# One full-height subtraction below block 0, later masks, another order of SyncE's DMAs and an inverse from blocks of 8 rows, in a delta-rule attention kernel with a feed-forward layer

## The chip, the cores and the metric

The kernel runs on one core of a Trainium2 chip. The metric is the device time of one execution in microseconds (us). Each kernel is run several times and the median is taken; a profiled execution beside them gives the trace. Engines are named as in the profile: PE (matmuls), PEld (its weight loads), DVE (vector), ACT (scalar), POOL (GpSimd), SP (SyncE, which here only issues DMAs).

## The reference

Two layers, one after the other: a delta-rule attention over 4 batches x 8 heads, 768 positions of 48 elements, then a feed-forward layer with a quick GELU on 3072 tokens of 384 elements (the heads side by side) with 2048 hidden units.

```python
k_n = k / (norm(k) + 1e-06)
for t in range(S):
    y[:, :, t] = einsum('bhd,bhde->bhe', q[:, :, t], state)
    v_old = einsum('bhde,bhd->bhe', state, kt)
    state = state + bt * einsum('bhd,bhe->bhde', kt, vt - v_old)
...
h = x @ w_in
g = h * (1.0 / (1.0 + exp(-1.702 * h)))
out = g @ w_out
```

q, k, v and beta are float32. The two weight matrices arrive as 8-byte floats, and the kernel turns them into float32 on the chip.

## The kernel before, in words

**Tiling.** The sequence is cut into 6 chunks of 128 positions; a unit is one chunk of one batch (24 units, 8 heads each). Within a chunk the recurrence is a triangular system: with G the products of the keys among each other, U solves a unit lower triangular system with right side V. The chunk is cut into 4 blocks of 32 rows. `invert` (line 441) computes the inverses XB of the 32 x 32 diagonal blocks for all heads at once on DVE; then a unit's solve goes block by block: `solve` (623) forms U of a block (psU), `solved` (630) copies it out on ACT (US<-psU), `below` (610) multiplies it by G into the rows below (psR), `rest` (619) subtracts that from V on DVE (V<-V,psR). For block 0 `rest` makes two subtractions, 32 rows and 64 rows[...].

**Inverse.** It works in two 16-row halves: 15 rounds (line 471) of a multiply (P<-NT,YB) and a reduce (YB<-P) build the inverse of both halves at once, then eight larger multiply-reduce pairs (489, 498) build the block between them. Chunk 0 gets its input NT from PE over a transpose; chunk 1 gets it over DRAM: `prepare` (402) writes 32-column blocks of G to a buffer Nd in DRAM with four DMAs per unit, and reads them back as NT with one; both are on SP's queue. The first multiply of chunk 1's inverse is NT<-NT,bI. The inverse of chunk 0 ends with a transpose (YT) and four multiplies into XB; that of later chunks goes back through DRAM (Yd, XB<-Yd).

**Scores.** `scores` (565) turns q, multiplies with the keys (psQ), copies the result to M on ACT, and `select` (604) sets its upper triangle to zero on POOL with an affine select over 128 x 1024 elements ("mask" below).

**Order.** Most instructions are pinned to program order on their engine (the wrapper at line 102, which is why the profile gives line 102 for them). The parts of the start are interleaved by hand:

- lines 928-957, chunk 0: turned keys, norms, G, the inverse begun as a generator (947) and run at 952, 32 scalings of V on ACT (955, V<-V,zs), and the four masks (957). `warm(n)` (132) issues n dummy matmuls (ps_warm) that keep PE busy; `warm(NY)` inside the inverse (501) waits for a memset that DVE issues there.
- lines 994-1001, first pair of chunk 0's units: `hops` (959) yields calls of `together` (803), each a solve of one unit beside the product below of the other: (a,0); (b,0) with a's block 0; (a,1) with b's block 0; and so on. After each call come some steps of the weight conversion (`fill`, 294), a step of `preparing` (`keys`, 972: norms, turned keys, G and Nd/NT for chunk 1) and dummies.
- lines 1002-1009: outputs of the pair (`put_out`), then q and v loads of units 4 and 5 on SP.
- lines 1025-1039, second pair: the same, with `feed` (1013) giving PE parts of the feed-forward layer (`hidden`, 707: ph) in place of dummies after the third hop.
- lines 1045-1064: scores of unit 4 (V<-V,psQ among them), the rest of the `w_in` conversion, chunk 1's inverse (1057) with parts of ph between, then `w_out` conversions.
- line 1066: the steady part, `woven` (847), one step per unit, with feed-forward work taken from a queue.

The conversion (205) of a piece is five instructions on DVE and a Relu on ACT: a `tensor_scalar` into `w_in` or `w_out`, one into `tmp`, and three `scalar_tensor_tensor`. The feed-forward matmuls of a piece wait for it.

Of the kernel before, what the change touches and what calls it, by code (L numbers as in the profile page):

```python
# [18 lines left out]
def kernel(  # L19
# [32 lines left out]
    HB = 2  # L52
# [2 lines left out]
    GB = 8  # L55

    XR = DP - D
    NW, NA, NY, NU = 14, 3, 46, 11
    NQ = DFF // 4
    NPC = DFF // 8  # L60
    NS = C * C + C
# [67 lines left out]

    ones = ident.bitcast(mybir.dt.bfloat16)  # L130

    def warm(n, after=None):
        ps = ps_moe.tile([128, 256], F32, tag="moe", name="ps_warm")
        if after is not None:
            after(ps[:, 0:1], 0.0)
        for _ in range(n):
            pe.matmul(ps, lhsT=ones[:, 0:128], rhs=ones, start=True, stop=True)

# [263 lines left out]
    def prepare(n):  # L402

        c, b = units[n]
        turn(n)
        yield 0.6
        G = gram(n)
        if c == 1:
            Nd = dram.tile([H * C * BS], F32, tag="Nd", name="Nd", bufs=4)
            for blk in range(NB):  # L410
                u = slice(blk * BS, (blk + 1) * BS)
                sync(out=Nd.rearrange("(h p k) -> p h k", p=C, k=BS)[u], in_=G[u, :, u])
            yield 0.9
            sync(
                out=NT[b * NB * H : (b + 1) * NB * H].rearrange("d i k -> d (i k)"),
                in_=Nd.rearrange("(d r) -> d r", r=BS * BS),
            )
            yield 0.0
            return
        Nd = dram.tile([H * NS], F32, tag="Nd", name="Nd", bufs=4)  # L420
        dma = sync if c < 3 else nc.sync.dma_start
        dma(
            out=Nd.rearrange("(h r) -> h r", r=NS)[:, 0 : C * C].rearrange(
                "h (p k) -> p h k", k=C
            ),
            in_=G,
        )
        dma(
            out=NT[b * NB * H : (b + 1) * NB * H],
            in_=Nd.rearrange("(d r) -> d r", r=NS // NB)[:, 0 : BS * C].rearrange(  # L430
                "d (i k) -> d i k", k=C
            )[:, :, 0:BS],
        )
        yield 0.9
# [6 lines left out]
    def invert(c, b0=0, nb=B):  # L441

        np = nb * NB * H
        part = slice(b0 * NB * H, b0 * NB * H + np)
        N, Y = NT[part], YB[part]
        bc = bI[part, c].broadcast_to([np, BS, BS])
        tt, red = vec.tensor_tensor, vec.tensor_reduce
        if c > 0:
            tt(N, N, bc, op=ALU.mult)
            yield 0.0  # L450
        HS = BS // 2

        def dots(o, a, b, ny, nx, nk, negate):

            P = wk.tile([128, ny, nx, nk], F32, tag="P", name="P")[part]
            tt(P, a, b, op=ALU.mult)
            red(o, P, axis=AX.X, op=ALU.add, negate=negate)

        def halves(t):

            return [t[:, s * HS : (s + 1) * HS, s * HS : (s + 1) * HS] for s in range(2)]


        Yf = Y.rearrange("p j i -> p (j i)")
        Nf = N.rearrange("p i k -> p (i k)")
        step = HS * BS + HS

        def diag(t, off, dims):
            return bass.AP(t.tensor, t.offset + off, [t.ap[0], [step, 2]] + dims)

        for i in range(1, HS):
            P = wk.tile([128, 2, i, i], F32, tag="P", name="P")[part]
            tt(
                P, diag(Nf, i * BS, [[0, i], [1, i]]), diag(Yf, 0, [[BS, i], [1, i]]),
                op=ALU.mult,
            )
            red(diag(Yf, i, [[BS, i]]), P, axis=AX.X, op=ALU.add, negate=True)
            yield 0.0


        X1 = N[:, 0:HS, HS:]
        if c <= 1:
            vec.tensor_copy(X1, halves(Y)[1].rearrange("p l i -> p i l"))
        else:
            act.activation(X1, halves(Y)[1].rearrange("p l i -> p i l"), ACT.Copy)
        A = N[:, 0:HS, 0:HS]
        N10, Y0 = N[:, HS:, 0:HS], halves(Y)[0]
        Q = 4
        for j in range(0, HS, Q):
            n = HS - j  # L490
            dots(
                A[:, j : j + Q, :],
                N10[:, :, j:].rearrange("p (o l) k -> p o l k", o=1).broadcast_to([np, Q, HS, n]),
                Y0[:, j : j + Q, j:].rearrange("p j (o k) -> p j o k", o=1).broadcast_to([np, Q, HS, n]),
                Q, HS, n, False,
            )
            yield 0.0
        for i in range(0, HS, Q):
            n = i + Q
            if c == 0 and i == HS - 3 * Q:  # L500
                warm(NY, vec.memset)
            dots(
                Y[:, 0:HS, HS + i : HS + i + Q],
                A[:, :, 0:n].rearrange("p j (o l) -> p j o l", o=1).broadcast_to([np, HS, Q, n]),
                X1[:, i : i + Q, 0:n].rearrange("p (o i) l -> p o i l", o=1).broadcast_to([np, HS, Q, n]),
                HS, Q, n, True,
            )
            yield 0.0
        if c == 0:
            T = wk.tile([128, BS, BS], F32, tag="P", name="YT")  # L510
            vec.transpose(T.rearrange("p d i -> p i d"), Y.rearrange("p j i -> p i j"))
            for b in range(B):
                XB = wk.tile([128, H, BS], F32, tag="XB", name="XB", bufs=4)
                tt(
                    XB, T[:, b * H : (b + 1) * H],
                    zs[:, 5, b].broadcast_to([128, H, BS]), op=ALU.mult,
                )
                inverse[b] = XB
                yield 0.0
            return  # L520
        YS = wk.tile([128, BS, BS], F32, tag="P", name="YS")[part]
        tt(YS, Y, bc, op=ALU.mult)
        dma = sync if c < 3 else nc.sync.dma_start
        groups = [range(b0, b0 + nb)]
        back = {}
        for bs in groups:
            for b in bs:
                back[b] = dram.tile([H * C, BS], F32, tag="Yd", name="Yd", bufs=4)
                dma(
                    out=back[b].rearrange("(p j) i -> p j i", j=BS),  # L530
                    in_=YS[(b - b0) * NB * H : (b - b0 + 1) * NB * H],
                )
            for b in bs:
                XB = wk.tile([128, H, BS], F32, tag="XB", name="XB", bufs=4)
                dma(out=XB, in_=back[b].rearrange("(h t) i -> t h i", h=H))
                inverse[c * B + b] = XB
        yield 0.0
# [7 lines left out]
    class Step:  # L545
# [63 lines left out]

        def below(self, blk, h, psR):  # L610
            r = slice(blk * BS, (blk + 1) * BS)
            for k in range(blk + 1, NB):
                u = slice(k * BS, (k + 1) * BS)
                pe.matmul(
                    psR[u, h, :], lhsT=self.G[r, h, u], rhs=self.U[r, h, :],
                    start=True, stop=True,
                )

        def rest(self, blk, psR):
            for u in (slice(BS, 2 * BS), slice(2 * BS, C)) if blk == 0 else (slice((blk + 1) * BS, C),):  # L620
                vec.tensor_tensor(self.V[u], self.V[u], psR[u], op=ALU.subtract)

        def solve(self, blk, h, psU):
            r = slice(blk * BS, (blk + 1) * BS)
# [328 lines left out]
    for s in pair:  # L953
        for h in range(H):
            act.mul(s.V[:, h, :], s.V[:, h, :], zs[:, 4, s.b, h : h + 1])
    for s in pair:
        s.select()

    def hops(a, b):

# [11 lines left out]
    def keys():  # L972

        def unit(n):
            yield from normalize_mixed(n)
            yield from prepare(n)

        begun[2 * B] = prepare(2 * B)

        def first(n):  # L980
            yield from normalize_mixed(n)
            next(begun[n])

        work = [unit(n) for n in range(B, 2 * B)] + [first(2 * B)]
        for t in range(22):
            for u, begin in enumerate((0, 3, 6, 10, 13)):
                s = t - begin
                if s >= 0 and s % 2 == 0:
                    next(work[u], None)
            yield  # L990
        for w in work:
            run(w)
# [2 lines left out]
    path = hops(*pair[:2])  # L995
    for i in range(2 * NB):
        together(*next(path))
        fill(1 if i < 2 else 2)
        if i > 0:
            ahead_of(preparing, 1)  # L1000
        warm(NU if i < 6 else NA)
    for n, s in enumerate(pair[:2]):
        put_out(s, 2 - n)
        load(len(KN) + n, ((KN, k),), other_queue)
        fill(1 + n)
    for n in range(B, B + 2):
        load(n, ((QP, q),), sync)
    for n in range(B, B + 2):
        load_values(n, sync)

    ffn = []

# [13 lines left out]
    for i in range(2 * NB):  # L1026
# [6 lines left out]
        ahead_of(preparing, 2)  # L1033
        if 3 <= i < 6:
            fetch_out(i - 3)
    for s in pair[2:]:
        put_out(s, 2)
        feed()
        fill(1)
    ffn.append(hidden(xTs[1], gTs[1], slice(0, NTH), 1.3, True))  # L1040
    xTs.pop(0), xTs.pop(1)
    load(B + 2, ((QP, q),), sync)
    for n in range(2 * B + 1, 2 * B + 1 + HB):
        load(n, ((KN, k),), sync)
# [55 lines left out]
```

## Time and profile before

| | us |
|---|---|
| median of 3 runs | 775.84 |
| lowest, highest | 775.49, 777.72 |
| the profiled execution | 775.34 |
| its span | 773.6 |
| PE busy | 747.1 (97% of the span) |
| DVE busy | 455.2 (59%) |
| ACT, POOL busy | 241.5, 126.5 |
| 96 subtractions V<-V,psR on DVE | 53.3 |
| 165 dummies ps_warm on PE | 23.6 |
| 20 masks M<-M on POOL | 25.4 |

The mean granted clock of PE was 0.976 of full speed. A busy time is the sum of the durations of an engine's instructions; PE's are modelled, so a full PE is not PE at its peak. A group's row gives the output and input tiles, partitions x elements, the count, the busy time, the mean duration of one in ns, and the idle time of the engine ahead of it with what ended it. The chain of waits goes back from the last instruction to what released each step. "issue" in it is time for which the profile shows no cause. Float32 matmuls appear as two records, called passes below.

### The profile page before, as it was taken

To read this page: it belongs to the slowest core of one execution; us is meant where nothing else is said; L and a number is where in the kernel's file an instruction comes from. 1 tells how busy PE (TensorE), PEld (TensorE's weight loads), DVE (VectorE), ACT (ScalarE), POOL (GpSimd) and SP (SyncE) were. 2 spreads that over 40 slices of the span, in tenths; PEclk is the share of its full clock that TensorE was granted. 3 is DMA by queue.
4 is the path that set the end of the run, shared out by engine and by line. 5 is a ranking of instruction groups with operands and counts; after the bars stand their busy time and mean duration, and the time that the engine had idled before them with its cause. 6 is when DMAs were issued, how large, how long until landed. Compare 5 with 4: busy or idle time off the path is not lost.

```text
span 773.6 us, 18836 instructions
## 1 busy us (share of the span) xinstructions
PE 747.1 (97%) x8165; PEld 560.1 (72%) x8165; DVE 455.2 (59%) x935; ACT 241.5 (31%) x535; POOL 126.5 (16%) x132
## 2 busy tenths in 40 slices
PE   7898999789999999999999999999999999999997
PEld 6677788456688678678678678678678677686774
DVE  6989879996975675665665665666665621000000
ACT  4564642343333223223223233233223123121110
POOL 6314200010220320220221211221210000000000
PEclk8598999999999999999999999999999999999999
DMA  9946640644342142042042042042030020000000
GB/s 167 176 65 174 145 87 1 170 114 97 76 109 56 25 105 56 22 107 57 22 101 63 22 100 65 22 97 66 22 77 13 22 44 2 16 12 1 25 1 21
DMA packets 130658, 50.73 MB, mean 66 GB/s; under 512 B 105408, under 2 KB 126016, under 8 KB 130576
## 3 DMA queue, kind: packets, MB, share of 16 engines
q1 hardware_dynamic: 128112, 41.08, 24.5%
q0 software_dynamic: 2464, 8.46, 4.5%
q8 instruction: 64, 1.05, 0.6%
q14 instruction: 18, 0.15, 0.1%
HBM read 32.08 MB, written 16.25 MB: 62 GB/s over the span
## 4 chain that ended last, share of the span: by engine, by line
PE 80%; DVE 14%; issue 2%; DMA 2%; ACT 2%; SPq 0%; POOL 0%; DVEq 0%; POOLq 0%; ACTq 0%
PE po L102 29%; PE ph L102 26%; PE psY L102 6%; PE psU L102 5%; PE psQ L102 4%; PE psG L102 4%; PE psT L102 3%; DVE P L102 3%; DVE w_out L102 2%; DVE tmp L102 2%; DVE YB L102 2%; PE psR L102 2%; PE ps_warm L102 2%; DVE V L102 1%; DVE NT L102 1%
## 5 line engine op out<-in xcount | busy, mean ns | idle before, releaser
L102 PE MATMUL po<-w_out,gT 128*128 128x384 f32 x768 | 266.1, 494 | 7.4 <-DVE w_out L102 7.4
L102 PE MATMUL ph<-xT,w_in 128*128 128x256 f32 x1152 | 261.2, 383 | 0.3
L102 PEld LDWEIGHTS ph<-xT,w_in 128*128 128x128 f32 x1152 | 214.8, 190 | 32.6 <-issue 1.7
L102 PEld LDWEIGHTS po<-w_out,gT 128*128 128x128 f32 x768 | 141.1, 190 | 98.8 <-DVE w_out L102 9.1
L102 DVE TENSOR_TENSOR V<-V,psR 64x384 f32<-64x384 f32 (+1 forms) x96 | 53.3, 555 | 189.8 <-PE psR L102 186.8
L102 ACT ACTIVATE gT<-ph 128x512 f32<-128x512 f32 x96 | 56.5, 596 | 142.3 <-PE ph L102 142.2
L102 DVE TENSOR_TENSOR P<-NT,YB 64x8 f32<-64x8 f32 (+31 forms) x190 | 89.4, 470 | 5.4
L102 ACT COPY US<-psU 32x384 f32<-32x384 f32 x92 | 43.2, 470 | 134.7 <-PE psR L102 120.5
L102 DVE TENSOR_REDUCE YB<-P 64x4 f32<-64x8 f32 (+31 forms) x190 | 80.9, 426 | 6.5
L102 PEld LDWEIGHTS psU<-V,XB 32*32 32x32 f32 x1536 | 57.7, 105 | 36.5 <-issue 27.7
L102 PE MATMUL psU<-V,XB 32*32 32x48 f32 x1536 | 68.6, 203 | 3.2 <-DVE V L102 2.4
L605 POOL TENSOR_SCALAR_AFFINE_SELECT M<-M 128x1024 f32<-128x1024 f32 x20 | 25.4, 1268 | 231.4 <-DVE M L102 167.4
L102 PE MATMUL psR<-US,G 32*32 32x48 f32 x2208 | 60.0, 203 | 0.6 <-ACT US L102 0.6
L102 PEld LDWEIGHTS psR<-US,G 32*32 32x32 f32 x2208 | 50.7, 105 | 1.9 <-ACT US L102 0.7
L102 PE MATMUL psQ<-QS,kT 48*128 48x176 f32 (+1 forms) x384 | 37.6, 341 | 3.0 <-ACT QS L102 3.0
L102 PE MATMUL psG<-kT 48*128 48x128 f32 x384 | 32.4, 306 | 3.4 <-ACT kT L102 2.2
L102 PEld LDWEIGHTS psQ<-QS,kT 48*128 48x128 f32 x384 | 31.1, 209 | 6.2 <-ACT QS L102 5.1
L102 DVE TENSOR_TENSOR P<-NT 64x256 f32<-64x256 f32 (+7 forms) x40 | 34.3, 859 | 0.4
L102 DVE TENSOR_REDUCE NT<-P 64x64 f32<-64x1024 f32 (+7 forms) x40 | 32.6, 815 | 1.4
L102 PEld LDWEIGHTS psG<-kT 48*128 48x128 f32 x384 | 27.4, 205 | 6.8 <-ACT kT L102 2.6
L102 ACT COPY o<-po 128x384 f32<-128x384 f32 x24 | 11.5, 479 | 61.7 <-issue 39.2
L102 ACT COPY M<-psQ 128x256 f32<-128x256 f32 x68 | 22.8, 376 | 22.7 <-DVE V L102 16.0
(99 smaller groups left out, 600.9 us busy)
## 6 DMA issues: line engine op xcount, KB each, us to landing
Nd<-G SPq DMA_DIRECT2D x16, 512.0 KB, 3.5
QP<-in_q_dram SPq DMA_DIRECT2D x24, 192.0 KB, 4.3
V<-in_v_dram SPq DMA_DIRECT2D x24, 192.0 KB, 3.1
out_dram<-o SPq DMA_DIRECT2D x24, 192.0 KB, 2.6
KN<-in_k_dram POOLq DMA_DIRECT2D x15, 192.0 KB, 3.6
NT<-Nd SPq DMA_DIRECT2D x20, 128.0 KB, 2.6
Yd<-YS SPq DMA_DIRECT2D x20, 128.0 KB, 2.4
XB<-Yd SPq DMA_DIRECT2D x20, 128.0 KB, 3.3
```

Of the source, the lines that this page charges most:

```text
L102: return lambda *a, **kw: tc.keep_in_program_order(op(*a, **kw))
L605: (pool if self.n < B else nc.gpsimd).affine_select(out=self.M, in_=self.M, compare_op=ALU.is_gt, fill=0.0, base=0, pattern=[[0, H], [1, 1 ...
```

## The change

Six edits:

1. `below` for block 0 now also multiplies into rows 0 to 31 (the product of block 0 with itself), so that `rest` can subtract all 128 rows in one instruction; V's rows of block 0 are not read again.
2. The masks of chunk 0 move: those of the first pair are put behind a POOL copy that reads the last column of YB (the end of the inverse's last reduce), that of the third unit behind a copy that reads XB of the fourth batch, and those of the second pair are issued after hops 3 and 5 of the first pair.
3. For chunks 0 and 1 the inverse starts from 8-row blocks: 7 rounds on four blocks at once, one copy, and four multiply-reduce pairs of 512 elements that join 8-row blocks to 16-row ones; the rest is as before.
4. The dummies before chunk 0's first solve are 34 in place of 46, and are no longer held by a memset in the inverse.
5. SP's order: NT of a unit is issued one step of `preparing` later, behind the next unit's Nd; q and v of unit 4 go behind the sixth hop of the second pair, those of unit 5 behind that pair. Within a step of `preparing` the later units come first.
6. In the first pair's first two hops `fill` takes two steps in place of one.

```diff
-    NW, NA, NY, NU = 14, 3, 46, 11
+    NW, NA, NY, NU = 14, 3, 34, 11
...
                 sync(out=Nd.rearrange("(h p k) -> p h k", p=C, k=BS)[u], in_=G[u, :, u])
+            yield 0.0
             yield 0.9
...
-        for i in range(1, HS):
-            P = wk.tile([128, 2, i, i], F32, tag="P", name="P")[part]
+        QS = HS // 2 if c <= 1 else HS
+        nb8 = BS // QS
...
+        for i in range(1, QS):
+            P = wk.tile([128, nb8, i, i], F32, tag="P", name="P")[part]
...
+        if QS < HS:
+            shape = [np, QS, QS, QS]
+            first, second = ([slice(s * HS + o, s * HS + o + QS) for s in range(2)] for o in (0, QS))
+            vec.tensor_copy(
+                diag(Nf, QS, [[BS, QS], [1, QS]], 2), diag(Yf, QS * BS + QS, [[1, QS], [BS, QS]], 2)
+            )
+            for a, b in zip(first, second):
+                dots(
+                    N[:, a, a],
+                    N[:, b, a].rearrange("p (o l) k -> p o l k", o=1).broadcast_to(shape),
+                    Y[:, a, a].rearrange("p j (o k) -> p j o k", o=1).broadcast_to(shape),
+                    QS, QS, QS, False,
+                )
+                yield 0.0
+            for a, b in zip(first, second):
+                dots(
+                    Y[:, a, b],
+                    N[:, a, a].rearrange("p j (o l) -> p j o l", o=1).broadcast_to(shape),
+                    N[:, a, b].rearrange("p (o i) l -> p o i l", o=1).broadcast_to(shape),
+                    QS, QS, QS, True,
+                )
+                yield 0.0
...
-            if c == 0 and i == HS - 3 * Q:
-                warm(NY, vec.memset)
...
-            for k in range(blk + 1, NB):
+            for k in range(blk + 1 if blk else 0, NB):
...
+        def under(self, blk):
+
+            return slice((blk + 1) * BS if blk else 0, C)
+
         def rest(self, blk, psR):
-            for u in (slice(BS, 2 * BS), slice(2 * BS, C)) if blk == 0 else (slice((blk + 1) * BS, C),):
-                vec.tensor_tensor(self.V[u], self.V[u], psR[u], op=ALU.subtract)
+            u = self.under(blk)
+            vec.tensor_tensor(self.V[u], self.V[u], psR[u], op=ALU.subtract)
...
-    for s in pair:
+    pool.tensor_copy(landed, YB[:, 0, BS - 1 : BS])
+    for s in pair[:HB]:
         s.select()
+    pool.tensor_copy(landed, inverse[B - 1][:, 0, 0:1])
+    warm(NY)
...
-        for t in range(22):
-            for u, begin in enumerate((0, 3, 6, 10, 13)):
+        for t in range(24):
+            for u, begin in reversed(list(enumerate((0, 3, 6, 10, 13)))):
...
-        fill(1 if i < 2 else 2)
+        fill(2)
+        if i in (3, 5):
+            pair[HB + (i - 3) // 2].select()
...
-    for n in range(B, B + 2):
-        load(n, ((QP, q),), sync)
-    for n in range(B, B + 2):
-        load_values(n, sync)
...
         if 3 <= i < 6:
             fetch_out(i - 3)
+        if i == 5:
+            load(B, ((QP, q),), sync)
+            load_values(B, sync)
...
+    load(B + 1, ((QP, q),), sync)
+    load_values(B + 1, sync)
     load(B + 2, ((QP, q),), sync)
```

More of the change, by code (lines that the diff above doesn't have):

```diff
@@ L130, with warm @@
     ones = ident.bitcast(mybir.dt.bfloat16)
-    def warm(n, after=None):
+    def warm(n):
         ps = ps_moe.tile([128, 256], F32, tag="moe", name="ps_warm")
-        if after is not None:
-            after(ps[:, 0:1], 0.0)
         for _ in range(n):
@@ L465, in invert, with diag @@
         Nf = N.rearrange("p i k -> p (i k)")
-        step = HS * BS + HS
-        def diag(t, off, dims):
-            return bass.AP(t.tensor, t.offset + off, [t.ap[0], [step, 2]] + dims)
-        for i in range(1, HS):
-            P = wk.tile([128, 2, i, i], F32, tag="P", name="P")[part]
+        QS = HS // 2 if c <= 1 else HS
+        nb8 = BS // QS
+        def diag(t, off, dims, n=nb8):
+            return bass.AP(t.tensor, t.offset + off, [t.ap[0], [BS // n * (BS + 1), n]] + dims)
+        for i in range(1, QS):
+            P = wk.tile([128, nb8, i, i], F32, tag="P", name="P")[part]
             tt(
```

## The prediction

> **What bounds the kernel now.** I read the page first: the span is 773.6 us and PE is busy for 97% of it, so most of the run can only shift as a block, and the place to look is where PE still waits. The table of busy time by stage shows that place (columns: stage, its length, then busy time and instruction count of PE, weight load, DVE, ACT, POOL; then granted clock, DMA share, GB/s).
>
> ```profile
> 90.00:100.00 10.00, 10.00 (x132) 8.44 (x127) 9.68 (x15) 6.89 (x15) 0.00 (x0) 1.00 0.47 118
> 100.00:110.00 10.00, 10.00 (x59) 8.52 (x58) 5.70 (x18) 4.46 (x10) 1.64 (x2) 1.00 0.33 85
> ...
> 130.00:140.00 10.00, 7.46 (x31) 5.40 (x30) 9.72 (x16) 3.28 (x6) 1.91 (x1) 1.00 0.43 88
> 140.00:150.00 10.00, 6.82 (x43) 3.56 (x43) 9.69 (x19) 2.84 (x4) 0.00 (x0) 1.00 0.58 174
> 150.00:170.00 20.00, 17.98 (x182) 11.04 (x178) 19.31 (x45) 8.46 (x18) 2.95 (x2) 1.00 0.57 143
> ```
>
> From 80 to 130 PE is full. From 130 to 170 it idles 2.54 + 3.18 + 2.02 = 7.7 us while DVE is at 97%: PE waits for converted `w_out`, and DVE comes late to it because it first does chunk 1's inverse (107 to 134). So the end of the run follows the time at which DVE starts that inverse, and what DVE does until the last `w_out` conversion at 171.6. The chain of waits says why the inverse starts at 107.27:
>
> ```profile
> 99.25 0.38 ACT xT L102
> ...
> 100.72 3.56 DMA Nd<-G
> 104.28 3.00 issue
> 107.27 1.24 DVE NT L102
> ```
>
> DVE had nothing to do for 3.00 us: the last quarter of NT was on its way. The timeline of SP's queue shows what held it:
>
> ```profile
> 75.00 5.01 SPq L102 DMA_DIRECT2D V<-in_v_dram  x2
> 80.53 3.52 SPq L102 DMA_DIRECT2D Nd<-G  x4
> 87.90 0.31 SPq L102 DMA_DIRECT2D NT<-Nd  x1
> 88.31 1.85 SPq L102 DMA_DIRECT2D Nd<-G  x4
> 95.38 0.31 SPq L102 DMA_DIRECT2D NT<-Nd  x1
> ...
> 99.27 2.76 SPq L102 DMA_DIRECT2D Nd<-G  x4
> 105.07 0.31 SPq L102 DMA_DIRECT2D NT<-Nd  x1
> ```
>
> Each NT load waits at the head of the queue until its Nd has landed, and the next unit's Nd stands behind it. The four G were copied by ACT at 72.1, 78.9, 83.7 and 89.8, so the last Nd left 8.4 us after its data was there.
>
> **What the skill says.** (1) "SBUF — State Buffer", Who interferes with whom: a DVE instruction with two SBUF inputs and a GpSimd instruction that reads SBUF exclude each other, and the second to issue blocks completely; a reduce never takes part. The trace agrees: a mask at 34.19 made a 256-element multiply take 1.16 us, where its like at 33.49 took 0.42, so 0.74 us was lost.
>
> ```profile
> 34.19 1.09 POOL L102 TENSOR_SCALAR_AFFINE_SELECT M<-M 128x1024 f32<-128x1024 f32 x1 [1.97 <-ACT M L102]
> 34.40 1.16 DVE L102 TENSOR_TENSOR P<-NT 128x256 f32<-128x256 f32 x1
> ```
>
> (2) "TensorEngine Tiling (Array Packing)", 32×32 Mode and Key Properties: tiles are fixed by the partitions read and written, and different tiles run in parallel. The trace agrees: 48 psR passes to three tiles took 0.88 us at 151.89, 16 psU passes to one tile 0.83 at 44.20. In chunk 0's hop at 46.28 one psU and three psR, four tiles of one row group, start together, and 16 such rounds are 0.042 us apart:
>
> ```profile
> 46.34 0.20 PE L102 MATMUL psU<-V,XB 32*32 32x48 f32 x1
> 46.35 0.21 PE L102 MATMUL psR<-US,G 32*32 32x48 f32 x3
> 46.39 0.20 PE L102 MATMUL psU<-V,XB 32*32 32x48 f32 x1
> ```
>
> So four tiles cost no more than one.
>
> **The change, part by part.**
>
> *The product of block 0 with itself.* Eight more matmuls a step, 24 steps, in tile (rows 0-31, columns 0-31). In the steady part (20 steps) no other product in the same call uses that tile: the solve beside it is of block 2. Cost 0; bounds 0 and 0.67 us a step (16 passes of 42 ns if they were serial). Only in the second hop of each of chunk 0's two pairs is a solve of block 0 in that same tile: there +0.67 us of PE, two times.
>
> *One subtraction for two.* DVE saves 0.557 + 0.03 us a step. After 171.6 PE waits for next to nothing (2.2 us of waits in 600 us), so 20 or so of the 24 are worth 0 (at best 0.5 us together). Those near 47, 49, 74 and 77 lie among the hops, below. The one at 155.08 is in the DVE-bound stretch: -0.58.
>
> *First inverse.* Before: 15 rounds from 16.61 to 27.49, 10.9 us. After: seven rounds of 4 to 196 products; by start-to-start times of the old rounds, interpolated by size, 0.39 + 0.42 + 0.46 + 0.51 + 0.60 + 0.69 + 0.79 = 3.86; a copy of 128 elements, 0.3 (that of 256 took 0.50; bounds 0.15 and 0.5); four pairs of 512 elements at 0.72 + 0.69 = 1.42, 5.7. Sum 9.85: -1.05 us. The mask's 0.74 goes too. The XB multiplies could start at 41.9 in place of 43.7; but two masks now start as the last reduce ends (39.9), 1.2 us each (26.57: 1.21), and the second holds the multiplies to about 42.4. None of this reaches PE: the first copy US<-psU stands behind 32 scalings of V on ACT, which end at 45.08 in both kernels.
>
> ```profile
> 43.70 1.46 ACT L102 ACTIVATE V<-V,zs 128x48 f32<-128x48 f32 x6
> 45.08 0.47 ACT L102 COPY US<-psU 32x384 f32<-32x384 f32 x1
> ```
>
> So worth 0 by itself. DVE's free time goes into an idle of 1.60 us at 45.7, which takes the conversion that is now issued one hop earlier.
>
> *Fewer dummies.* 46 take 6.64 us from 37.27; by 0.12 us each for warm ones, 34 end at about 42.4, before psU needs PE at 43. The gap is 0.6 us, too short to matter for the clock (it stayed at 1.00 after the 0.29 us gap before; a 1.78 us gap at 59.7 came before a clock of 0.50). Cost 0; if the clock did fall, about 1 us in the first hop.
>
> *Hops of chunk 0.* First pair: the hop can begin at 45.65 (copy done) in place of 46.28 and is 0.67 longer: 0. DVE runs one more conversion per early hop (+0.96) and one subtraction less for two hops (-1.16); ACT gets a Relu ahead of the second US copy, which then ends near 51.3 in place of 49.8, and the subtraction at 52.18 stays about there. One of the later masks runs after `rn` (57) and can hold a DVE conversion for 0.6. Second pair: +0.67 in PE at 72, less 0.20 of a wait for V and 0.68 of a wait for kT (its Relu is issued a hop earlier). I take +0.1 for both pairs; bounds -0.9 and +1.2. PE is then full up to 99, so this sum carries on.
>
> *SP's order.* The last Nd is issued when G is there, 90.9 to 92.8, lands 3.56 later (96.4); behind it on SP stand NT of the third unit, then QP (0.8) and V (0.7) of one unit, then the last NT at about 97, landed by 99.2 (2.2 at the median). DVE needs it at 104.4: no more wait. What was moved past: QP and V of unit 4 leave SP at 94 in place of 73 to 80; by the page's median QP lands in 4.3, at 98.3, and psT needs it at 100.6. Two us of room; with the 7.4 us seen under load it is 0.8 late. The second xT leaves earlier than 105, for free. psQ now follows psT without three ph between, and waits for two ACT copies, to 102.4: as before.
>
> *Start of chunk 1's inverse.* V<-psQ ends at 104.28 + 0.1, so NT x bI starts at 104.4 in place of 107.27: -2.9. But unit 4's mask (104.94 to 106.03 now, in DVE's idle) then meets DVE: it waits for the first multiply, 104.4 to 105.6, takes 1.09, and the next multiply waits: +1.0 (bounds 0, if DVE keeps the port, and 1.2). The inverse itself: -1.05 as above. Then the subtraction, -0.58.
>
> Sum: -2.9 + 1.0 - 1.05 - 0.58 = -3.5 us at 171.6. PE has 7.7 us of idle to give there, so DVE still sets the pace and all of it reaches the end. Against the profiled execution's 775.34 (span 773.6 and 1.74 around it) that is 771.8; this execution lies 0.5 below the median of the runs, 775.84, so the forecast is **772.3**.
>
> **Rivals.** *No collision (770.2).* Masks find gaps, the hops gain 0.5 to 0.9: 3.5 + 1.0 + 0.6 + 0.5 = 5.6. For it: PE's saved waits at 77. Against: the 0.74 at 34.4. *Another wait takes the place of NT (774.5).* QP lands late, or the hops lose 1.2 to the serial tile and a mask: 3.5 - 1.2 - 1.0 = 1.3. For it: a QP load took 7.4 us in a busy stretch. *Products not hidden (slower, 785.7).* If the fourth tile's passes were serial in the steady part, where PE is full, 20 x 0.67 = 13.4 less 3.5. It decides from 0.18 us a step on. Against: four tiles of one row group already run in the time of one, at 46.28; for it: no row shows the four and a solve of another block at once.
>
> **Chances.** Forecast 0.50, no collision 0.19, another wait 0.25, serial products 0.06. A measurement of this kernel can tell about 0.3% (2.3 us) from no change, so faster means under 773.5. The forecast gives nearly all its 0.50 to faster, the second 0.19, the third a quarter: 0.74; same 0.20; slower 0.06. The range runs from the no-collision case with all bounds good, 769.4, to the third with its bad ones, 775.3.
>
> **What would show it.** Right: NT x bI on DVE between 103.5 and 105.5 without a 3 us idle before it; its rounds done in 9.9 us; PE idle from 130 to 170 of some 5 us; a multiply near 106 of over 1 us; the second hop 0.67 us longer and the steady psR calls 0.88 still, 64 passes. Wrong: psR calls of 1 us and more after 171; QP or V the last thing before psQ; DVE idle again before NT; PE's phases from 80 to 99 over 1 us later than now.

## The result, and the profile after

The kernel after takes 774.84 us (median of 14 runs, 772.42 to 776.18), the kernel before beside it 775.95 (14 runs). The ratio is 0.9982, 95% interval 0.9973 to 0.9992: a gain of 1.1 to 1.4 us, within the 0.3% that the prediction calls the same. The forecast was 772.3, so it had the sign and overrated the size two and a half to three times.

The two profiled executions, 775.34 before and 775.35 after (spans 773.6 and 773.7), differ by nothing. So the traces have to be compared stage by stage, not by their ends. The table of stages of the kernel after (columns as in the prediction) already shows where it went wrong:

```profile
100.00:110.00 10.00, 9.06 (x71) 7.80 (x67) 7.60 (x21) 4.45 (x12) 1.97 (x2) 1.00 0.57 122
130.00:140.00 10.00, 9.16 (x40) 7.02 (x38) 5.37 (x9) 3.23 (x6) 0.18 (x1) 1.00 0.64 131
140.00:150.00 10.00, 6.85 (x29) 3.59 (x29) 9.76 (x20) 3.46 (x5) 1.85 (x1) 0.83 0.33 94
150.00:170.00 20.00, 18.68 (x204) 11.59 (x204) 19.45 (x43) 8.43 (x18) 2.84 (x2) 1.00 0.61 162
```

DVE, which was busy for 9.72 of the 10 us from 130 to 140, is busy for 5.37 now: the engine that was to set the pace stands still for almost half of that stretch. PE's idle from 130 to 170 is 5.31 us, the "some 5" that the prediction expected, but for another reason: PE's own ph reach 2.5 us further into the stretch (last gT at 137.64, before 135.14). DVE's timeline says which instruction stands and for what (start, length, engine, tiles; in brackets the idle time ahead and what ended it):

```profile
105.39 1.22 DVE L102 TENSOR_TENSOR NT<-NT,bI 128x1024 f32<-128x1024 f32 x1
106.64 0.93 DVE L102 TENSOR_TENSOR P<-NT,YB 128x4 f32<-128x4 f32 x1
...
131.24 1.22 DVE L102 TENSOR_TENSOR YS<-YB,bI 128x1024 f32<-128x1024 f32 x1
...
134.29 0.36 DVE L102 TENSOR_SCALAR tmp<-raw 128x384 int32<-128x384 int32 x1
139.18 0.55 DVE L102 TENSOR_REDUCE ssq<-ksq 128x8 f32<-128x384 f32 x1 [4.53 <-ACT ksq L102]
```

POOL's mask of unit 4 in the same view:

```profile
106.14 1.42 POOL L624 TENSOR_SCALAR_AFFINE_SELECT M<-M 128x1024 f32<-128x1024 f32 x1 [4.18 <-ACT M L102]
```

The 3.00 us ahead of NT<-NT,bI are gone; the collision with a mask is there (0.93 us for 4 elements; those of 2 and 8 elements in before take 0.16 and 0.17); and the inverse ends 2.2 us earlier than before (YS at 131.24, before at 133.44). Then 4.53 us are lost in one wait. The chain of waits tells what that wait hangs on:

```profile
103.52 0.04 issue
103.56 1.46 PE psQ L102 x16
105.03 32.59 PE ph L102 x150
137.64 0.05 ACT gT L102
...
138.13 0.60 ACT w_out L102
138.74 0.42 ACT ksq L102
139.18 0.55 DVE ssq L102
```

Before, the chain went through DVE's inverse. Now it runs over 32.59 us of PE's ph, its last gT on ACT, a Relu and a square behind that on ACT, and only then to DVE. I call this the gate: ACT works in order, and the Relu of the second `w_out` piece (a) and the square ksq (b) stand behind the last gT; DVE's reduce ssq needs (b). The Relu's own input was written by DVE at 132.85; it started at 138.13. The Trainium skill has the rule ("PSUM — Partial Sum Buffer", Engine vs sequencer instructions): the queue of ScalarE is strict FIFO; this trace agrees, with 5 us between input and start.

The same place in the kernel before, ACT first and then DVE:

```profile
135.14 0.60 ACT L102 ACTIVATE gT<-ph 128x512 f32<-128x512 f32 x1 [1.93 <-PE ph L102]
135.63 0.61 ACT L102 ACTIVATE w_out<-w_out,low 128x384 int32<-128x384 int32 x1
136.14 0.51 ACT L102 ACTIVATE ksq<-KN 128x384 f32<-128x384 f32 x1
```

```profile
136.50 0.36 DVE L102 TENSOR_SCALAR tmp<-raw 128x384 int32<-128x384 int32 x1
136.77 0.54 DVE L102 TENSOR_REDUCE ssq<-ksq 128x8 f32<-128x384 f32 x1
```

ksq was done at 136.65 and DVE came for it at 136.77. No wait shows, so no list of waits names the gate; but its slack was 0.12 us. In this execution DVE's inverse and PE's ph were two paths of nearly equal length, and a shorter inverse alone could gain 0.12 us.

### The profile page after: what moved, and what is told of

It is laid out like the page before. It is cut to its first block, busy times and chain, and to the rows that moved or that the text cites. A ratio compares the mean times of both kernels' runs of the same rounds, so it can differ in the third digit from the quotient of the medians.

```text
span 773.7 us, 19538 instructions
## 1 busy us (share of the span) xinstructions
PE 749.6 (97%) x8537; PEld 563.1 (73%) x8537; DVE 439.9 (57%) x896; ACT 240.8 (31%) x535; POOL 129.1 (17%) x134
## 4 chain that ended last, share of the span: by engine, by line
PE 87%; DVE 7%; ACT 3%; issue 1%; DMA 1%; POOL 0%; SPq 0%; DVEq 0%; POOLq 0%; ACTq 0%
PE ph L102 31%; PE po L102 30%; PE psY L102 6%; PE psU L102 5%; PE psQ L102 4%; PE psG L102 4%; PE psT L102 3%; PE psR L102 3%; DVE w_out L102 2%; DVE tmp L102 2%; PE ps_warm L102 1%; ACT V L102 1%; DVE P L102 1%; DVE V L102 1%; DVE YB L102 0%
## 5 line engine op out<-in xcount | busy, mean ns | idle before, releaser
L102 DVE TENSOR_TENSOR V<-V,psR 128x384 f32<-128x384 f32 (+2 forms) x72 | 40.1, 557 | 195.4 <-PE psR L102 190.3
L102 DVE TENSOR_TENSOR P<-NT,YB 64x8 f32<-64x8 f32 (+26 forms) x178 | 85.8, 482 | 4.9
L102 PEld LDWEIGHTS psU<-V,XB 32*32 32x32 f32 x1536 | 58.7, 105 | 35.6 <-issue 27.6
L102 DVE TENSOR_REDUCE YB<-P 64x4 f32<-64x8 f32 (+27 forms) x178 | 77.2, 434 | 6.1
L102 PE MATMUL psR<-US,G 32*32 32x48 f32 x2576 | 62.7, 204 | 0.8 <-ACT US L102 0.8
L102 PEld LDWEIGHTS psR<-US,G 32*32 32x32 f32 x2576 | 53.3, 104 | 2.3 <-ACT US L102 1.2
L102 DVE TENSOR_TENSOR P<-NT 64x256 f32<-64x256 f32 (+7 forms) x44 | 36.3, 825 | 0.5
L102 DVE TENSOR_REDUCE NT<-P 64x64 f32<-64x1024 f32 (+7 forms) x44 | 35.3, 803 | 1.5
L87 POOL DMA_DIRECT2D KN<-in_k_dram x13 | 12.4, 953 | 105.9 <-PE psY L102 96.9
```

Of the source, the lines that this page charges most:

```text
L87: dma(out=dst[n % len(dst)][:, :, 0:D], in_=src[b, :, c * C : (c + 1) * C, :].rearrange("h p d -> p h d"),)
L102: return lambda *a, **kw: tc.keep_in_program_order(op(*a, **kw))
```

## The experiments

Each kernel ran beside the kernel before on the same chip, whose medians were 776.01 (e1 to e4), 776.44 (e5 to e8) and 775.93 (e9 to e12). Three theories are held against each other: G is the gate; D is the forecast's own step, that DVE's inverse sets the end; H, a rival, is that the gain was lost in the start and the hops.

| run | edit | median us | ratio to before (95%) |
|---|---|---|---|
| after | | 774.84 | 0.9982 (0.9973 to 0.9992) |
| e1 | after, gate open | 769.51 | 0.9927 (0.9905 to 0.9949) |
| e2 | before, gate open | 774.76 | 0.9991 (0.9976 to 1.0006) |
| e3 | before, SP's new order | 774.97 | 0.9996 (0.9975 to 1.0018) |
| e4 | after, SP's old order | 775.21 | 0.9982 (0.9968 to 0.9995) |
| e5 | after, gate open, SP's old order | 769.64 | 0.9923 (0.9901 to 0.9946) |
| e6 | after, gate open, inverse ahead of psQ | 769.62 | 0.9925 (0.9904 to 0.9947) |
| e7 | after, psQ behind a ph group | 773.41 | 0.9962 (0.9949 to 0.9974) |
| e8 | after, first inverse as before | 775.63 | 0.9989 (0.9975 to 1.0002) |
| e9 | after, 3.75 us more in the inverse | 775.27 | 0.9984 (0.9969 to 0.9999) |
| e10 | e1, 3.75 us more in the inverse | 772.60 | 0.9950 (0.9932 to 0.9968) |
| e11 | after, two subtractions, no product of block 0 with itself | 775.37 | 0.9991 (0.9975 to 1.0006) |
| e12 | after, conversions as before | 773.61 | 0.9974 (0.9958 to 0.9990) |

An interval is some 3 us wide, so only differences of 2 us and more are told by the times alone; below that I go by the traces, each of which is one execution.

**e1, e2: opening the gate.**

```diff
     for i in range(25):
         ahead_of(inverting, 1)
-        feed()
+        if i < 21:
+            feed()
     run(inverting)
     fill(5)
+    feed(2)
+    fill(5)
+    feed(2)
+    fill(5)
```

> Kernel after, with one edit: the last two ph groups of the hidden layer, and so their gT on ACT, are put behind the first w_out conversions in program order (one conversion, a group, one conversion, a group, one conversion). Theory G (gate): after the inverse DVE stands idle for 4.5 us (134.7 to 139.2) because its next operand comes from ACT behind the last gT, which PE sets at 137.6. With the edit the idle goes, DVE-bound work ends 2.5 to 4 us earlier, limited by the 5.3 us that PE idles from 130 to 170: 771.5 (770.5 to 772.5). Theory D (the forecast's step: DVE's inverse already sets the end): no gain, 774.8. Theory H (the gain was lost in the start and the hops, PE being later by 1.5 us from 12 us on): PE's work sets the end, gain 0 to 0.5, 774.5.

> Kernel before, with the same edit as e1. Theory G: here the inverse ends at 134.6 and the last gT starts at 135.1, and DVE reaches the operand behind it at 136.8 when it is just there, so the edit is worth 0 to 0.5 us: 775.7. If it gains as much as in e1, 3 us, the edit is good for another reason than the gate, and theory G falls. Theories D and H: 775.9.

e1 takes 769.51, 5.3 us less than after by the medians (4.3 by the ratios) and below G's range; D and H fall as the main cause. e2 gains 1.25 us by the medians and 0.7 by its ratio, which is not told from nothing and far from e1's gain. It moves the same work of PE, so that move alone is not what gains: the edit is worth something only where the inverse ends early. A version that moves only ACT's two instructions ahead of the last gT, with PE's order as it is, was not run. ACT's timeline of e1 (this execution, at 774.64 the slowest of its six, lies 3.6 us later than after's, since its PE clock stood at 0.54 from 45 to 60) shows the Relus between the gTs, and DVE's the reduce without a wait:

```profile
136.07 0.60 ACT L102 ACTIVATE gT<-ph 128x512 f32<-128x512 f32 x1 [1.93 <-PE ph L102]
136.84 0.61 ACT L102 ACTIVATE w_out<-w_out,low 128x384 int32<-128x384 int32 x1 [0.17 <-DVE w_out L102]
138.72 0.60 ACT L102 ACTIVATE gT<-ph 128x512 f32<-128x512 f32 x1 [1.26 <-PE ph L102]
139.21 0.61 ACT L102 ACTIVATE w_out<-w_out,low 128x384 int32<-128x384 int32 x1
141.25 0.60 ACT L102 ACTIVATE gT<-ph 128x512 f32<-128x512 f32 x1 [1.43 <-PE ph L102]
```

```profile
142.54 0.36 DVE L102 TENSOR_SCALAR tmp<-w_out 128x384 int32<-128x384 int32 x1
142.82 0.55 DVE L102 TENSOR_REDUCE ssq<-ksq 128x8 f32<-128x384 f32 x1
```

From V<-psQ to the psG on PE that ends the `w_out` stage it is 65.2 us in e1 (108.07 to 173.25) and 69.6 in after (104.46 to 174.02): 4.4 us, the wait that is gone. The other 0.9 us of the 5.3 by the medians lie within the interval.

**e3, e4, e5: SP's order.** e3 is edit 5 alone in the kernel before; e4 takes it out of after, e5 out of e1.

```diff
-            yield 0.0
             yield 0.9
...
-        for t in range(24):
-            for u, begin in reversed(list(enumerate((0, 3, 6, 10, 13)))):
+        for t in range(22):
+            for u, begin in enumerate((0, 3, 6, 10, 13)):
```

(e4 and e5; the loads of q and v go back to their old places as well.)

> Kernel before, with only the new order of SyncE (the NT load a step later, the units in reverse, QP and V moved). NT x bI should start at 103.5 to 104.5 instead of 107.27 in the trace. Theory G: the inverse ends 2 to 3 us earlier and DVE idles for that time before the operand behind the last gT; time 775.9 (775.4 to 776.3). Theory D: the 2.9 us less 1.0 for a mask reach the end: 774.0 (773.0 to 774.2).

> Kernel after, with SyncE's old order put back; the rest as in after. NT x bI should start 2 to 3 us later than 105.4. Theory G: this fits in the 4.5 us for which DVE idles after the inverse: 774.8 (774.3 to 775.3). Theory D: plus 1.9 to 2.9: 777.0.

> Kernel after with the edit of e1 (the last two ph groups behind the first w_out conversions) and, at once, SyncE's old order of e4. Theory G: with the gate open DVE sets the pace again, so the late NT counts now: 769.5 + 2.5 = 772.0 (771.0 to 773.0), where in e4, with the gate shut, it cost nothing that could be seen. If e1's gain had nothing to do with passing on the inverse: 769.5 again.

e3: NT<-NT,bI follows V<-psQ at once, but DVE then waits for ksq:

```profile
142.62 0.55 DVE L102 TENSOR_REDUCE ssq<-ksq 128x8 f32<-128x384 f32 x1 [2.14 <-ACT ksq L102]
```

The wait was moved, as G says. The time alone hardly decides: its interval runs from 774.1 to 777.4, G's 775.9 lies inside and D's 774.0 at the lower edge. e4 shows no loss, which G allows, but in its trace NT is not late: NT<-NT,bI follows V<-psQ at once (109.48). e5 missed: 772.0 was expected and it is 769.64, the same as e1. The trace says why. NT<-NT,bI follows V<-psQ at once here too, with the old order of SP:

```profile
102.51 0.42 DVE L102 TENSOR_TENSOR V<-V,psQ 128x96 f32<-128x96 f32 x2 [1.81 <-PE psQ L102]
103.11 0.42 DVE L102 TENSOR_TENSOR V<-V,psQ 128x96 f32<-128x96 f32 x2 [0.18 <-PE psQ L102]
103.45 1.22 DVE L102 TENSOR_TENSOR NT<-NT,bI 128x1024 f32<-128x1024 f32 x1
```

```profile
95.18 2.82 SPq L102 DMA_DIRECT2D Nd<-G  x4
99.28 0.31 SPq L102 DMA_DIRECT2D NT<-Nd  x1
```

From the start of the last unit's four Nd to the NT behind them it took 4.10 us here, 3.38 in e4, 4.36 in e2 and 5.80 in the trace of before (99.27 to 105.07). With the old order, then, four traces show an idle ahead of NT of 3.00, 1.29 (e2, the same program as before up to there), 0 and 0 us. The 3.00 on which the prediction built its largest term hung on one execution's DMA times; which idle is usual in the kernel before, two traces don't say. So neither e4 nor e5 can test what an early NT is worth. e9 and e10 test what the end of the inverse is worth.

**e9, e10: the same work added with the gate shut and open.** This tests the gate without any DMA: three products of 128 x 1024 that nothing reads, on DVE, in chunk 1's inverse.

```diff
+        if c == 1:
+            for _ in range(3):
+                P = wk.tile([128, BS, BS], F32, tag="P", name="P")
+                tt(P, N, Y, op=ALU.mult)
         HS = BS // 2
```

> Kernel after with three products of 128x1024 on DVE added to chunk 1's inverse, right behind NT x bI; nothing reads them. DVE's inverse ends 3 x 1.25 = 3.75 us later. Theory G: DVE stands idle for 4.53 us behind the inverse, waiting for ACT's work behind the last gT, so this is free: 774.8 (774.3 to 775.5). Theory D (the inverse's end sets the pace, as the forecast has it): 778.6.

> The kernel of e1 (gate open) with the same three products in the inverse. Theory G: with the gate open DVE doesn't idle, so they now cost nearly all of their 3.75 us: 769.5 + 3.5 = 773.0 (772.0 to 773.5). If PE alone set the end in e1: 769.5 to 770.

e9 takes 775.27, the same as after within its interval; D's 778.6 (a ratio of 1.003) is excluded. Its trace shows the wait eaten up, from 4.53 to 0.77, and from V<-psQ to the reduce it is 34.72 us in both kernels (102.33 to 137.05, in after 104.46 to 139.18). Behind the reduce this one execution takes 2.5 us longer to that psG than after's, with PE's clock at 0.52 from 150 to 160.

```profile
137.05 0.55 DVE L102 TENSOR_REDUCE ssq<-ksq 128x8 f32<-128x384 f32 x1 [0.77 <-ACT ksq L102]
```

e10 takes 772.60, 3.1 more than e1 by the medians (1.8 by the ratios), and from NT<-NT,bI to that psG it is 68.0 us (104.88 to 172.88) where e1 has 64.2: the full 3.75. ACT now waits 3.94 us for DVE where it waited 0.17 in e1, and DVE doesn't wait for ACT:

```profile
136.48 0.61 ACT L102 ACTIVATE w_out<-w_out,low 128x384 int32<-128x384 int32 x1 [3.94 <-DVE w_out L102]
```

So the end of the inverse counts only with the gate open. With e1 and e2, this pair settles why the shorter inverse was lost.

**e7, e12: what moved the gate.** In before a group of ph (1.39 us from its start to that of psQ; the 1.15 in the expectation below is too short) stands on PE between psT and psQ of unit 4; in after it doesn't, and PE waits (before, then after):

```profile
100.53 0.60 PE L102 MATMUL psT<-ident,QP 128*128 128x128 f32 x4
100.97 1.46 PE L102 MATMUL ph<-xT,w_in 128*128 128x256 f32 x6
102.36 1.46 PE L102 MATMUL psQ<-QS,kT 48*128 48x176 f32 x16
```

```profile
102.03 0.60 PE L102 MATMUL psT<-ident,QP 128*128 128x128 f32 x4
103.56 1.46 PE L102 MATMUL psQ<-QS,kT 48*128 48x176 f32 x16 [0.94 <-ACT QS L102]
```

The loop that feeds PE there ends when the last `w_in` piece is converted. Edit 6 puts the conversions two steps ahead, so it ends one round sooner. e7 puts the group back; e12 takes edit 6 out.

```diff
         t += 1
+    feed()
     run(preparing)
```

```diff
-        fill(2)
+        fill(1 if i < 2 else 2)
         if i in (3, 5):
```

> Kernel after with one edit: a ph group of PE (1.15 us) put back between psT of unit 4 and psQ, where before has it, so that PE doesn't wait 0.94 us for QS. Theory G: PE's last ph, which is the gate, comes 0.9 us earlier, and DVE's later start of 0.2 is hidden: 773.9 (773.4 to 774.4). Theory D: 775.0, since DVE starts the inverse 0.2 later.

> Kernel after with one conversion step, not two, in each of the first two hops, as before. The w_in conversions are then a step later, and by that a ph group of PE stands again between psT of unit 4 and psQ. Theory G: PE no longer waits 0.94 us before psQ, and its last ph comes 0.9 earlier, as in e7: 773.7 (773.2 to 774.5), unless the first two hops cost more. The forecast's price for this edit was 0: 774.8.

e7 takes 773.41 and e12 773.61: 1.4 and 1.2 less than after by the medians, 1.6 and 0.6 by the ratios, where 0.9 was expected. Both lie where G has them. In both traces the last gT follows psT by 34.6 us, as in before, where after has 35.6, and DVE's wait at ssq is 3.23 and 3.25 us in place of 4.53. The intervals alone don't tell these two from after; the traces show the gate earlier by 1.0 us.

**e8, e11: the first inverse, and the product of block 0 with its single subtraction.**

```diff
-        QS = HS // 2 if c <= 1 else HS
+        QS = HS // 2 if c == 1 else HS
```

```diff
-            for k in range(blk + 1 if blk else 0, NB):
+            for k in range(blk + 1, NB):
...
-            u = self.under(blk)
-            vec.tensor_tensor(self.V[u], self.V[u], psR[u], op=ALU.subtract)
+            for u in (slice(BS, 2 * BS), slice(2 * BS, C)) if blk == 0 else (slice((blk + 1) * BS, C),):
+                vec.tensor_tensor(self.V[u], self.V[u], psR[u], op=ALU.subtract)
```

> Kernel after with the first inverse of chunk 0 in 15 rounds of 16-row halves as before; chunk 1's stays at 8 rows. The forecast and theory G: worth 0, since ACT's 32 scalings of V cover it: 774.8 (774.3 to 775.3). Rival: if the first hop stood on DVE's inverse, 1.05 us and the masks behind it later: 776.0.

> Kernel after without the product of block 0 with itself and with two subtractions below block 0, as before. One such pair stands behind the gate, among the w_out conversions (0.58 us); the others are worth 0 to 0.5 together, and the hops give back up to 2 x 0.67 us of PE. Forecast's prices: 774.8 + 0.6 (774.0 to 775.9). If the products of block 0 were serial in the 20 steady steps: 774.8 - 13.

e8, 775.63, lies between the two expectations (774.8 and 776.0) and its interval holds both: not decided by the time. Its trace has V<-psQ at 101.92, not later than after's (104.46), which speaks for 0, though weakly. e11, 775.37, is where the forecast's prices put it, though its interval would hold no change too; the 13 us less that serial products would have meant are excluded. The pair among the `w_out` conversions takes 1.15 us from start to start there (155.64 to 156.79), the single one 0.47 in after.

**e6: the version that the experiments point to.** With the gate open, the next wait on DVE is 1.81 us for psQ, with NT landed. The edit below is made together with e1's, whose loop then feeds PE 20 times instead of 21.

```diff
     run(preparing)
-    run(first.scored)
+    feed()
     inverting = invert(1)
+    ahead_of(inverting, 4)
+    run(first.scored)
```

> Kernel after with the edit of e1, one ph group put back between psT and psQ, and the first four steps of chunk 1's inverse on DVE ahead of V<-psQ. In the trace of after DVE waits 1.81 us for psQ at 104.46 with NT landed, and PE 0.94 us for QS before psQ. Theory G: both go, the inverse starts 1.8 us earlier and PE's last ph 0.9 earlier; of the 3.0 us for which PE still idles from 140 to 170 in e1, up to 1.8 go: 767.7 (767.2 to 769.0). If PE rather than DVE sets the end once the gate is open: 768.6.

It takes 769.62, above G's range: a miss, and no gain over e1 that can be seen. In its trace the inverse does start ahead of V<-psQ (99.51 and 101.91), but a wait of 1.10 us for ksq is back at ssq. From psT to the psG that ends the stage it is 66.6 us, 1.0 less than in e1; then, after an idle of 1.45 us, PE's clock falls (0.83 from 160 to 170), and from that psG to the end it is 600.9 us, 1.3 more than in e1. Versions e1, e5 and e6 beat both kernels, e1 by 6.5 us against before in the medians and 5.7 by the ratio.

## Why the prediction was wrong

The step that failed stands under "Start of chunk 1's inverse" and its sum: "PE has 7.7 us of idle to give there, so DVE still sets the pace and all of it reaches the end." PE had that idle, but behind its last ph, not ahead of it. DVE's first stop after the inverse hangs on PE's last ph by way of ACT. Of the 2.95 us that the sum moves the inverse's end (-2.9 + 1.0 - 1.05), 0.12 could pass. What the runs show in its place is the gate: 4.53 us of wait in after, none with it open, 5.3 us of gain (4.3 by the ratios); 3.75 us of added work free with it shut (e9) and paid with it open (e10).

Most of the signs that the prediction named for being right came true all the same: NT<-NT,bI at 105.39 without an idle ahead of it, PE idle for 5.31 us, psR calls of 0.88. None of them looks at what DVE does behind the inverse.

The steps one by one:

- *NT's 3.00 us of idle go*: so in the trace, but the 3.00 was one execution's; others with the old order show 0 to 1.29, and undoing the order costs nothing that can be seen (e4, e5).
- *psQ "to 102.4: as before"*: wrong. The prediction saw that three ph no longer stand between, and that psQ waits for ACT's two copies, but priced it at nothing, because it looked at when DVE gets psQ. What it costs is PE's: 0.94 us, and the last gT comes 35.6 us after psT instead of 34.6 (102.03 to 137.64; before 100.53 to 135.14). As PE's ph are the gate, that is a loss: without it the gate comes 1.0 us earlier in e7's trace, and its median is 1.4 lower.
- *Collision with unit 4's mask, +1.0*: right, 0.76 (0.93 against 0.17).
- *Inverse, -1.05*: right. From NT<-NT,bI to YS it takes 25.85 us in place of 26.17, and 0.76 of that is the collision: -1.08.
- *One subtraction among the conversions, -0.58*: right, -0.68, and it lies behind the gate, so it is kept.
- *First inverse, 0*, and *hops, +0.1*: not contradicted. From chunk 0's last psQ to unit 4's psT it is 65.29 us (36.74 to 102.03), before 65.34; but other executions of the same program as after up to there have 63.74 (e6) to 70.50 (e1, with the fall of the clock named above), so a step of this size is not told.
- *Fourth tile hidden*: right. The steady calls with 64 passes take no longer than those with 48, so the rival at 785.7 is out:

```profile
154.04 0.88 PE L102 MATMUL psR<-US,G 32*32 32x48 f32 x64
```

- *After 171.6 PE waits for next to nothing*: right in effect. From psG to the end of the span it is 599.7 us, before 600.8; the other traces spread from 598.1 to 601.7, e11 with two subtractions at the low end, so nothing of this is put down to the subtractions. PE's clock covers the 1.1 us: it falls at this psG in before and not in after, and the two calls take 1.6 us longer there (before, then after):

```profile
172.78 1.49 PE L102 MATMUL psG<-kT 48*128 48x128 f32 x16 [1.51 <-ACT kT L102]
174.21 2.86 PE L102 MATMUL po<-w_out,gT 128*128 128x384 f32 x4
```

```profile
174.02 1.16 PE L102 MATMUL psG<-kT 48*128 48x128 f32 x16 [1.45 <-ACT kT L102]
175.11 1.56 PE L102 MATMUL po<-w_out,gT 128*128 128x384 f32 x4
```

The sum from unit 4's psT on, as the two traces have it: +1.0 (the gate, 0.94 of it psQ's wait), -1.3 (from the last gT to psG: 37.64 to 36.38), -1.1 (psG to the end) = -1.4. In these two executions 1.5 us of a later start hide it (below); the medians show -1.1. Of the -1.3, 0.68 is the subtraction and 0.09 the slack at ssq; some 0.5 in small gaps between DVE's instructions is not explained. The last -1.1 is the fall of the clock. All three traces with before's program at this place have it (before, e2, e3), and of the eleven others only e6 and e8. So most of the measured gain may lie there, and whether the change makes this fall rarer, or the executions only happened so, stays open.

The rival "another wait takes the place of NT (774.5)" gave the right time by luck, with the wrong wait: it named a late QP and the hops. QP left SP at 95.44 and psT was not held by it.

H, the loss in start and hops, falls as the main cause: after's trace is 1.5 us late at chunk 0's last psQ (36.74, before 35.19), but other kernels with after's program up to there have 34.80 (e9), 35.08 (e5) and 37.06 (e11), so it differs from one execution to the next, at the place shown in the last section. Whether the change has a part in it stays open: the three traces with before's program up to there have 34.78 to 35.19, the eleven with after's 34.80 to 37.06.

## What to carry to other kernels

When work is taken off the engine that sets the pace, look for the next instruction on it whose operand comes from another engine, follow that operand back in program order through in-order queues, and measure its slack: ready time against the time at which it is used. A wait of zero in a trace can be a tie of two paths, as the 0.12 us of slack were here, and then neither of them is worth shortening alone. And a wait that hangs on a DMA's round trip should be read from more than one execution before it is priced.

## What the runs showed of the hardware that was not expected

In these traces PE's granted clock fell after short idles, and at the start it stayed down for long though PE was busy. There PE stands before the last psD; the clock then drops, in after a little sooner:

```profile
11.24 0.76 PE L102 MATMUL psD<-kT 48*32 48x32 f32 x65 [1.60 <-issue]
11.93 1.16 PE L102 MATMUL psG<-kT 48*128 48x128 f32 x16
13.77 2.56 PE L102 MATMUL psG<-kT 48*128 48x128 f32 x16 [0.68 <-ACT G L102]
```

```profile
11.83 0.82 PE L102 MATMUL psD<-kT 48*32 48x32 f32 x65 [2.43 <-issue]
12.58 2.08 PE L102 MATMUL psG<-kT 48*128 48x128 f32 x16
15.34 2.56 PE L102 MATMUL psG<-kT 48*128 48x128 f32 x16 [0.68 <-ACT G L102]
```

(before, then after). The first psG call takes 1.16 us or 2.08, and that with the later psD is the 1.5 us. From 14 to 40 us the clock is 0.50 in both, with PE busy for 22.7 and 22.0 of the 26 us and no gap over 0.7 us. The Trainium skill ("TensorE: Matmul & The Clock Gate", What's actually happening) gives about 3.4 us of idle for the fall and of activity for the return. The traces differ from the first figure, and at the start from the second, and they decide here: falls follow idles of 1.24 us (e1, at 10.49) to 2.56 (e11, at 12.23), one of 2.24 in before (147.82) is followed by none, and the idle of 1.45 us ahead of the psG that ends the `w_out` stage is followed by a fall in e6 and e8 and by none in after and e1. The return at the start came only in the stretch of dummies without gaps (0.50 from 38 to 40 and 0.91 from 40 to 42 in before). What in the activity ahead of it is too little for the clock was not tried.
